# An elementwise kernel with its own semaphores: first loads ahead of the entry barrier, a single engine's wait at the end, y kept whole in SBUF

## The chip, the cores and the metric

The kernel runs on one core of a Trainium2 chip. The metric is the device time in microseconds (us) of the whole execution. Each execution also has a span, from its first recorded instruction to its last. The time is longer than the span by a part that the trace does not show: 1.77 us in the profiled run of the kernel before. This change moves that part too, to 1.33 us.

Engines are called as in the profile: PE (TensorE), DVE (VectorE), ACT (ScalarE), POOL (GpSimd), SP (SyncE).

## The reference

```python
B, S, D = 1024, 16, 512          # x, y: [B, S, D] bf16; gamma: [D] bf16
def reference(x, y, gamma):
    return x + gamma * y
```

It reads two tensors of 16.8 MB and writes one: 50.33 MB in all, for one multiply and one add per element.

## The kernel before

Each of the 128 partitions holds 128 rows of 512 elements. The work is cut in four pieces of 32 rows (4 MB each). A tile framework allocates six buffers, places the waits, and opens and closes the program with rounds in which all engines meet (barriers).

```python
    nc.gpsimd.dma_start(out=gamma_row[:], in_=gamma.unsqueeze(0))
    nc.vector.memset(ones_row[:], 1.0)
    nc.tensor.matmul(gamma_ps[:], ones_row[:], gamma_row[:], start=True, stop=True)  # gamma to all partitions
    nc.vector.tensor_copy(out=gamma_sb[:], in_=gamma_ps[:])
    io_pool = ctx.enter_context(tc.tile_pool(name="io", bufs=SLOTS))                 # SLOTS = 6
    # ... cut: lists xs and ys, the call for manual scheduling ...
    for c in range(n_pieces):                                                        # 4 pieces
        r = slice(c * PIECE, (c + 1) * PIECE)
        xt = io_pool.tile([P, PIECE, D], dt, tag="io")
        yt = io_pool.tile([P, PIECE, D], dt, tag="io")
        nc.sync.dma_start(out=xt[:], in_=xv[:, r, :])      # SP's queue
        nc.scalar.dma_start(out=yt[:], in_=yv[:, r, :])    # ACT's queue
        # ... cut: DVE: yt = yt * gamma_sb, then yt = xt + yt; xt and yt go into the lists ...
    for c in range(n_pieces):
        r = slice(c * PIECE, (c + 1) * PIECE)
        eng = nc.sync if c % 2 == 0 else nc.scalar
        eng.dma_start(out=ov[:, r, :], in_=ys[c][:])
```

(The small tiles' allocations are cut.) Six buffers hold three pieces of x and of y. The loads of the fourth piece wait for buffers: x3 is issued after the first add (40.2 us), y3 after the second (59.6 us). Below, x0 to x3, y0 to y3 and out0 to out3 are the loads and stores of the four pieces.

## Time and profile before

| | before |
|---|---|
| time, median of 3 runs (range) | 123.46 us (123.09 to 123.53) |
| profiled run: time, span | 123.22 us, 121.45 us |
| first 32 KB packet starts, last one ends | 1.76 us, 119.95 us |
| 32 KB packets: number, usual duration, in flight | 1,536, 1.213 us, 16 |
| DVE busy | 70.4 us |

The packet rows are read from the DMA packet records of the trace, which have the start, duration, size and queue of every packet. They do not name the DMA engine: with 16 packets in flight, and the page's share of 16 engines, every 16 packets are counted here as one for each engine.

These are lines of the page of the kernel before. "DMA" and "GB/s" have one value for each of 40 equal slices of the span (3.04 us each); a 9 means 90% or more busy. Part 4 is the chain of work that ended last.

```profile
span 121.5 us, 80 instructions
...
PE 0.6 (0%) x1; PEld 0.1 (0%) x1; DVE 70.4 (58%) x10; POOL 0.8 (1%) x5
...
DMA  5899999999999999999999999989898989898992
GB/s 173 378 486 389 475 399 464 399 464 421 442 432 432 410 453 410 453 399 464 410 453 410 453 410 453 345 345 518 356 507 356 507 356 507 367 496 389 475 410 108
...
## 4 chain that ended last, share of the span: by engine, by line
DMA 53%; DVE 29%; ACTq 0%; issue 0%
```

The DMA row is at 9 or 8 from the second slice to the last but one: the DMA engines bound this kernel. A sum confirms it: 1,536 packets / 16 x 1.213 us = 116.5 us, at 432 GB/s, of the 118.19 us from the first packet to the end of the last. The shortest of the 1,536 packets takes 1.211 us, so the usual duration is also the best that this trace shows; whether such a packet could be faster is not shown. Taken at this rate, there is little to win in the middle. What can be won lies before the first packet, after the last one, and in slow packets. The latter come to 1.55 us per engine over the usual duration, most of it in two places: the first packet of each engine (0.60 us over), and one round at 77.6 us (0.75 us over).

The head of the timeline (start in us, duration in us, engine; "q" is the sequencer that issues; a merged row's duration reaches from its first issue to the end of its last):

```profile
0.74 1.37 ACTq L57 DMA_DIRECT2D yt<-in_y_dram  x3
0.74 1.33 SPq L56 DMA_DIRECT2D xt<-in_x_dram  x3
...
1.22 0.61 POOL L43 DMA_DIRECT2D gamma_row<-in_gamma_dram  x1 [0.78 <-POOLq L85]
...
11.05 0.69 DVE L47 CAST gamma_sb<-gamma_ps 128x512 bf16<-128x512 f32 x1 [10.06 <-PE gamma_ps L46]
```

Both queues issue their first load at 0.74 us, after the entry barrier. The first packet starts at 1.76 us, 1.0 us later.

The end, from the view of the closing line of the program (L96), with columns count, shortest/median/longest ns, first and last start in us:

```profile
L96 SPq EVENT_SEMAPHORE  x7: 17/28/28, 120.3 to 121.4; - x7
L96 POOLq EVENT_SEMAPHORE  x4: 17/17/17, 120.7 to 121.3; - x4
...
L96 SPq DRAIN  x3: 7/7/7, 120.6 to 120.9; - x3
...
L96 DVEq EVENT_SEMAPHORE  x2: 21/21/21, 120.9 to 121.4; - x2
...
L96 POOLq EVENT_SEMAPHORE_RANGE_CLEAR  x1: 136/136/136, 121.0 to 121.0; - x1
```

SP's wait for the stores is over at 120.3 us. Then come drains, rounds of semaphores among the five engines and a clear of a range of semaphores, up to 121.4 us.

### The profile page before, as it was taken

The numbers are of one execution on the slowest core, as the hardware profiler recorded it, in microseconds if no ns is written. First come the engines' busy times: TensorE is split into PE (matmuls) and PEld (weight loads), VectorE is DVE, ScalarE is ACT, GpSimd is POOL, SyncE is SP. The second block draws the span as 40 slices with busy tenths as digits, with TensorE's granted clock in tenths as the row PEclk, the third lists the DMA queues.
The fourth block names the chain that finished last, engine by engine and source line by source line (L and its number), as shares of the span: only waits on it lengthen the run. The fifth ranks groups of instructions, "written<-read, shape, count | busy, mean of one in ns | idle before, by whom it ended". The sixth has DMA issues, their size and how long they took to land.

```text
span 121.5 us, 80 instructions
## 1 busy us (share of the span) xinstructions
PE 0.6 (0%) x1; PEld 0.1 (0%) x1; DVE 70.4 (58%) x10; POOL 0.8 (1%) x5
## 2 busy tenths in 40 slices
PE   0001000000000000000000000000000000000000
PEld 0000000000000000000000000000000000000000
DVE  0002000499999399999679999907999990000000
POOL 2000000000000000000000000000000000000000
DMA  5899999999999999999999999989898989898992
GB/s 173 378 486 389 475 399 464 399 464 421 442 432 432 410 453 410 453 399 464 410 453 410 453 410 453 345 345 518 356 507 356 507 356 507 367 496 389 475 410 108
DMA packets 1760, 50.33 MB, mean 414 GB/s; under 512 B 224, under 2 KB 224, under 8 KB 224
## 3 DMA queue, kind: packets, MB, share of 16 engines
q10 hardware_dynamic: 864, 25.17, 48.7%
q1 hardware_dynamic: 864, 25.17, 48.6%
q0 software_dynamic: 32, 0.00, 0.0%
HBM read 33.56 MB, written 16.78 MB: 414 GB/s over the span
## 4 chain that ended last, share of the span: by engine, by line
DMA 53%; DVE 29%; ACTq 0%; issue 0%
DMA yt<-in_y_dram 53%; DVE yt L58 14%; DVE yt L64 14%; ACTq L57 0%
## 5 line engine op out<-in xcount | busy, mean ns | idle before, releaser
L58 DVE TENSOR_TENSOR yt<-yt,gamma_sb 128x16384 bf16<-128x16384 bf16 x4 | 34.8, 8692 | 18.9 <-DMA yt<-in_y_dram 18.9
L64 DVE TENSOR_TENSOR yt<-xt,yt 128x16384 bf16<-128x16384 bf16 x4 | 34.8, 8692 | 0.1
L47 DVE CAST gamma_sb<-gamma_ps 128x512 bf16<-128x512 f32 x1 | 0.7, 692 | 10.1 <-PE gamma_ps L46 10.1
L44 DVE MEMSET ones_row<- 1x128 bf16 x1 | 0.2, 165 | 0.8 <-PEq L85 0.8
L46 PE MATMUL gamma_ps<-gamma_row,ones_row 1*128 1x512 bf16 x1 | 0.6, 579 | 10.4 <-DMA gamma_row<-in_gamma_dram 10.4
L43 POOL DMA_DIRECT2D gamma_row<-in_gamma_dram x1 | 0.6, 607 | 0.8 <-POOLq L85 0.8
L46 PEld LDWEIGHTS <-ones_row 1*128 1x128 bf16 x1 | 0.1, 98 | 1.0 <-DVE ones_row L44 1.0
L85 POOL MEMSET const-bfloat16-1.0<- 128x1 bf16 x1 | 0.1, 97 | 0.0
L85 POOL MEMSET const-float32-0.0<- 128x1 f32 x1 | 0.1, 93 | 0.2 <-issue 0.2
L85 POOL MEMSET const-float32-1.0<- 128x1 f32 x1 | 0.1, 94 | 0.0
L85 POOL MEMSET const-uint8-127<- 128x1 uint8 x1 | 0.1, 94 | 0.0
## 6 DMA issues: line engine op xcount, KB each, us to landing
yt<-in_y_dram ACTq DMA_DIRECT2D x4, 4096.0 KB, 32.1
xt<-in_x_dram SPq DMA_DIRECT2D x4, 4096.0 KB, 40.5
out_dram<-yt SPq DMA_DIRECT2D x2, 4096.0 KB, 49.0
out_dram<-yt ACTq DMA_DIRECT2D x2, 4096.0 KB, 31.1
gamma_row<-in_gamma_dram POOLq DMA_DIRECT2D x1, 1.0 KB, 9.2
```

The lines of the kernel that those rows point to most:

```text
L43: nc.gpsimd.dma_start(out=gamma_row[:], in_=gamma.unsqueeze(0))
L44: nc.vector.memset(ones_row[:], 1.0)
L46: nc.tensor.matmul(gamma_ps[:], ones_row[:], gamma_row[:], start=True, stop=True)
L47: nc.vector.tensor_copy(out=gamma_sb[:], in_=gamma_ps[:])
L58: nc.vector.tensor_tensor(out=yt[:], in0=yt[:], in1=gamma_sb[:, None, :].to_broadcast([P, PIECE, D]), op=mybir.AluOpType.mult,)
L64: nc.vector.tensor_tensor(out=yt[:], in0=xt[:], in1=yt[:], op=mybir.AluOpType.add)
L85: nc = _bacc.Bacc("TRN2", target_bir_lowering=False, num_devices=1)
```

## The change

The intent is to put the DMA-free parts at both ends out of the way.

- The tile program is closed empty at the start; the kernel is written behind it with its own semaphores (counters on which engines wait), each of which the waiting engine counts back to zero.
- The first five loads (gamma, x0, x1, y0, y1) are moved to the front of the program, ahead of the entry barrier.
- At the end only SP waits, for the four stores.
- y has room for all four pieces in SBUF (the memory in which the buffers lie), x for two; gamma is loaded by ACT instead of POOL.

```diff
+def _take(sem, n, eng):
+    return eng.wait_ge(sem, n).then_inc(sem, -n)
...
+    tc.close()
+    tc.compile()
...
-    io_pool = ctx.enter_context(tc.tile_pool(name="io", bufs=SLOTS))
+    y_sb = nc.alloc_sbuf_tensor("y_sb", [P, rows, D], dt).ap()
+    xs = [nc.alloc_sbuf_tensor(f"x{i}", [P, PIECE, D], dt).ap() for i in range(2)]
...
-    nc.gpsimd.dma_start(out=gamma_row[:], in_=gamma.unsqueeze(0))
+    first.append(load(nc.scalar, gamma_row, gamma.unsqueeze(0), s_gamma))
...
+    first.append(load(nc.sync, xs[0], xv[:, piece(0), :], s_x[0]))
+    first.append(load(nc.sync, xs[1], xv[:, piece(1), :], s_x[1]))
+    _take(s_sp, 1, nc.sync)                                    # first add done
+    load(nc.sync, xs[0], xv[:, piece(2), :], s_x[2])
+    _take(s_sp, 1, nc.sync)                                    # second add done
+    load(nc.sync, xs[1], xv[:, piece(3), :], s_x[3])
+    nc.sync.dma_start(out=ov[:, piece(0), :], in_=y_sb[:, piece(0), :]).then_inc(s_out_sp, 16)
... (cut: out2 on SP; y0 to y3, then out1 and out3 on ACT; the two passes of DVE)
+    _take(s_out_sp, 32, nc.sync)
+    _take(s_out_act, 32, nc.sync)
+
+    main = nc.main_func.blocks[0].instructions
+    names = {i.ins.name for i in first}
+    for b in nc.main_func.blocks[1:]:
+        for i in [i for i in b.instructions if i.name in names]:
+            b.instructions.remove(i)
+    for k, i in enumerate(first):
+        main.insert(1 + k, i.ins)
```

More of the change, by code (lines that the diff above doesn't have):

```diff
@@ L1 @@
-from contextlib import ExitStack
 import concourse.bass as bass
@@ L5 @@
 from concourse import mybir
-from concourse._compat import with_exitstack
 PIECE = 32
-SLOTS = 6
-@with_exitstack
+MULT, ADD = mybir.AluOpType.mult, mybir.AluOpType.add
+def _take(sem, n, eng):
+    return eng.wait_ge(sem, n).then_inc(sem, -n)
 def kernel(
-    ctx: ExitStack,
     tc: tile.TileContext,
@@ L30 @@
     rows = N // P
-    n_pieces = rows // PIECE
+    n = rows // PIECE
     dt = xf.dtype
@@ L36 @@
     ov = of.rearrange("(p n) d -> p n d", p=P)
-    const_pool = ctx.enter_context(tc.tile_pool(name="const", bufs=1))
-    gamma_row = const_pool.tile([1, D], dt)
-    ones_row = const_pool.tile([1, P], dt)
-    gamma_sb = const_pool.tile([P, D], dt)
-    psum_pool = ctx.enter_context(tc.tile_pool(name="psum", bufs=1, space=bass.MemoryType.PSUM))
-    nc.gpsimd.dma_start(out=gamma_row[:], in_=gamma.unsqueeze(0))
-    nc.vector.memset(ones_row[:], 1.0)
-    gamma_ps = psum_pool.tile([P, D], mybir.dt.float32)
@@ L46 @@
-    nc.tensor.matmul(gamma_ps[:], ones_row[:], gamma_row[:], start=True, stop=True)
-    nc.vector.tensor_copy(out=gamma_sb[:], in_=gamma_ps[:])
-    io_pool = ctx.enter_context(tc.tile_pool(name="io", bufs=SLOTS))
-    xs, ys = [], []
-    ctx.enter_context(tc.manual_schedule())
-    for c in range(n_pieces):
-        r = slice(c * PIECE, (c + 1) * PIECE)
-        xt = io_pool.tile([P, PIECE, D], dt, tag="io")
-        yt = io_pool.tile([P, PIECE, D], dt, tag="io")
-        nc.sync.dma_start(out=xt[:], in_=xv[:, r, :])
-        nc.scalar.dma_start(out=yt[:], in_=yv[:, r, :])
-        nc.vector.tensor_tensor(
-            out=yt[:],
-            in0=yt[:],
-            in1=gamma_sb[:, None, :].to_broadcast([P, PIECE, D]),
-            op=mybir.AluOpType.mult,
-        )
-        nc.vector.tensor_tensor(out=yt[:], in0=xt[:], in1=yt[:], op=mybir.AluOpType.add)
-        xs.append(xt)
-        ys.append(yt)
@@ L67 @@
-    for c in range(n_pieces):
-        r = slice(c * PIECE, (c + 1) * PIECE)
-        eng = nc.sync if c % 2 == 0 else nc.scalar
-        eng.dma_start(out=ov[:, r, :], in_=ys[c][:])
+    gamma_row = nc.alloc_sbuf_tensor("gamma_row", [1, D], dt).ap()
+    ones_row = nc.alloc_sbuf_tensor("ones_row", [1, P], dt).ap()
+    gamma_sb = nc.alloc_sbuf_tensor("gamma_sb", [P, D], dt).ap()
+    y_sb = nc.alloc_sbuf_tensor("y_sb", [P, rows, D], dt).ap()
+    xs = [nc.alloc_sbuf_tensor(f"x{i}", [P, PIECE, D], dt).ap() for i in range(2)]
@@ new lines, with piece, load @@
+    gamma_ps = nc.alloc_psum_tensor("gamma_ps", [P, D], mybir.dt.float32).ap()
+    sem = nc.alloc_semaphore
+    s_gamma, s_ones, s_ps, s_dve = sem("s_gamma"), sem("s_ones"), sem("s_ps"), sem("s_dve")
+    s_x = [sem(f"s_x{c}") for c in range(n)]
+    s_y = [sem(f"s_y{c}") for c in range(n)]
+    s_sp, s_act = sem("s_sp"), sem("s_act")
+    s_out_sp, s_out_act = sem("s_out_sp"), sem("s_out_act")
+    def piece(c):
+        return slice(c * PIECE, (c + 1) * PIECE)
+    first = []
+    def load(eng, dst, src, s):
+        return eng.dma_start(out=dst, in_=src).then_inc(s, 16)
@@ new lines @@
+    first.append(load(nc.scalar, gamma_row, gamma.unsqueeze(0), s_gamma))
+    nc.vector.memset(ones_row, 1.0).then_inc(s_ones, 1)
+    _take(s_ones, 1, nc.tensor)
+    _take(s_gamma, 16, nc.tensor)
+    nc.tensor.matmul(gamma_ps, ones_row, gamma_row, start=True, stop=True).then_inc(s_ps, 1)
+    _take(s_ps, 1, nc.vector)
+    nc.vector.tensor_copy(out=gamma_sb, in_=gamma_ps).then_inc(s_dve, 1)
+    _take(s_dve, 1, nc.vector)
+    first.append(load(nc.sync, xs[0], xv[:, piece(0), :], s_x[0]))
+    first.append(load(nc.sync, xs[1], xv[:, piece(1), :], s_x[1]))
@@ new lines @@
+    _take(s_sp, 1, nc.sync)
[3 more added lines that the diff above has]
+    nc.sync.dma_start(out=ov[:, piece(0), :], in_=y_sb[:, piece(0), :]).then_inc(s_out_sp, 16)
+    _take(s_sp, 1, nc.sync)
+    nc.sync.dma_start(out=ov[:, piece(2), :], in_=y_sb[:, piece(2), :]).then_inc(s_out_sp, 16)
+    for c in range(n):
+        i = load(nc.scalar, y_sb[:, piece(c), :], yv[:, piece(c), :], s_y[c])
+        if c < 2:
+            first.append(i)
@@ new lines @@
+    _take(s_act, 1, nc.scalar)
+    nc.scalar.dma_start(out=ov[:, piece(1), :], in_=y_sb[:, piece(1), :]).then_inc(s_out_act, 16)
+    _take(s_act, 1, nc.scalar)
+    nc.scalar.dma_start(out=ov[:, piece(3), :], in_=y_sb[:, piece(3), :]).then_inc(s_out_act, 16)
+    for c in range(n):
+        yt = y_sb[:, piece(c), :]
+        _take(s_y[c], 16, nc.vector)
+        nc.vector.tensor_tensor(
+            out=yt, in0=yt, in1=gamma_sb[:, None, :].to_broadcast([P, PIECE, D]), op=MULT
+        ).then_inc(s_dve, 1)
+        _take(s_x[c], 16, nc.vector)
+        _take(s_dve, 1, nc.vector)
+        i = nc.vector.tensor_tensor(out=yt, in0=xs[c % 2], in1=yt, op=ADD)
+        if c == 0:
+            i.then_inc(s_sp, 1)
+        elif c == 1:
+            i.then_inc(s_dve, 1)
+            _take(s_dve, 1, nc.vector)
+            nc.vector.sem_inc(s_sp, 1)
+            nc.vector.sem_inc(s_act, 1)
+        else:
+            i.then_inc(s_sp if c == 2 else s_act, 1)
```

## The prediction

> **What bounds the kernel now.** The DMA engines. The page gives a span of 121.5 us, 50.33 MB moved, and a DMA row at 9 or 8 in nearly every slice; VectorE is busy 70.4 us (58%). In the trace's packet records the 1,536 packets of 32 KB take 1.21 us each, 16 at a time: 1536/16 x 1.213 = 116.5 us, or 432 GB/s.[...] The first such packet starts at 1.76 us, the last ends at 119.95 us: 118.2 us with 16 in flight throughout. Two things stretch them: the first packet of each engine takes about 1.9 us, and one round at 77.6 us, the first writes, about 1.95 us.
>
> - Ahead: the timeline has both first loads issued at 0.74 us, after the entry barrier (SP's waits show 0.7 us for it); first bytes about 1.0 us later.
> - Behind: SP's wait for the stores ends at about 120.3 us; then drains, two all-engine rounds of semaphores and a range clear run to 121.45 us: 1.15 us.
>
> **What the change does.**
> 1. Gamma, x0, x1, y0, y1 are issued before the entry barrier: SP's first at about 0.05 us in place of 0.74. Worth 0.65 to 0.7 us, all critical, since every transfer queues behind. Gamma now heads ACT's queue, so y0 is issued about 0.4 us after x0; x0 alone fills the engines meanwhile (at the end of this trace one queue alone keeps 1.21 us per packet). Cost about 0.
> 2. The closing drains, barriers and clear go; SP's waits with decrements stay (28 ns each). Worth 1.0 to 1.1 us, all critical.
> 3. y whole in SBUF: y3 is issued at once instead of at 59.6 us, x2 at 40.2 us instead of at once. x2 comes into SP's queue about when x1's last packet goes, and y2 fills any gap[...]. y3 lands about 2 us earlier (82.8 before), so the last add ends near 98 us instead of 100.3. No gain: out0 and out2 hold the engines then. Worth 0 +- 0.3 us.
> 4. Gamma by ACT, not POOL: off the path (VectorE waits from 11.7 to 22.8 us for y0).
> 5. VectorE's eight passes of 8.69 us: unchanged, hidden.
>
> **Sum.** 123.46 - 0.68 - 1.07 = 121.7 us; I say 121.65, range 121.0 to 122.3. Faster by over 2%: 0.11; within 2%: 0.87; slower: 0.02. Predicted span: 119.7 us.
>
> **What would show it right or wrong.**
> - Step 1: first DMA issue near 0.05 us, first 32 KB packet near 1.05 us.
> - Step 2: the trace ends within 0.2 us of the end of SP's wait.
> - Step 3: 32 KB packets still 1.21 us, first to last 118.2 us (117.7 to 118.7); DMA at 9 with no hollow slice near 41, 60 or 98 us.
>
> **What would make it wrong.** The 1.8 us between measured time and span of the same run (123.22 against 121.5) may hold work that changes with the program's start or ending. Reads and writes no longer meet in the same way, so slow rounds may be more, fewer or longer. If x2 or x3 comes late and both queues run dry, a hole of about 1 us appears. If the first access has a fixed start after launch whatever is issued, step 1 gives nothing.

## The result

| | before | after |
|---|---|---|
| time, median of 4 runs (range) | 123.41 us (123.09 to 123.53) | 121.23 us (121.17 to 121.28) |
| profiled run: time | 123.22 us | 121.17 us |
| its span | 121.45 us | 119.84 us |
| time minus span | 1.77 us | 1.33 us |
| first 32 KB packet starts | 1.76 us | 1.01 us |
| from there to the end of the last | 118.19 us | 118.37 us |
| from there to the end of the span | 1.50 us | 0.46 us |

The ratio is 0.9827 (95% interval 0.9808 to 0.9846). By the ratio the change is faster by 1.5 to 1.9%, inside the "within 2%" to which the prediction gave 0.87.

The page of the changed kernel, the same lines as above (slices of 3.00 us):

```profile
span 119.8 us, 90 instructions
...
PE 0.6 (0%) x1; PEld 0.1 (0%) x1; DVE 70.3 (59%) x10; POOL 0.2 (0%) x4
...
DMA  8999998989898989898999989999999999989994
GB/s 274 427 427 448 405 470 361 514 350 525 350 525 350 525 350 525 350 492 383 437 437 427 448 372 405 405 394 481 394 481 394 448 427 438 437 383 470 405 470 197
...
## 4 chain that ended last, share of the span: by engine, by line
DVE 7%; issue 0%
```

The first and the last slice are fuller; in between the row is as full as before. Part 4 needs care. It says "DVE 7%" and nothing of DMA, though the kernel is as DMA-bound as before. In both kernels the chain's last piece is the last add, which ends 21 us before the end of the span in the kernel before and 25 us here; the stores behind it are in neither chain. From the last add the view went back to 0.68 us in the kernel before, through the loads, but here it stopped at once: a wait here is an instruction of its own that also lowers the semaphore, and the view did not follow the chain back through it. For the bound, the DMA row and the packets are to be read, not the chain.

The head of the timeline of the changed kernel:

```profile
0.00 0.86 SPq L62 DMA_DIRECT2D x<-in_x_dram  x2
0.12 0.53 ACTq L62 DMA_DIRECT2D gamma_row<-in_gamma_dram  x1
...
0.69 2.75 ACTq L62 DMA_DIRECT2D y_sb<-in_y_dram  x4
...
5.42 0.69 DVE L71 CAST gamma_sb<-gamma_ps 128x512 bf16<-128x512 f32 x1 [2.56 <-DVEq L12]
```

Its waits, from the view of line L12, the wait in `_take` (columns as for the end of before):

```profile
L12 DVEq EVENT_SEMAPHORE  x15: 21/21/21, 5.3 to 86.2; - x15
L12 SPq EVENT_SEMAPHORE  x5: 17/17/17, 41.8 to 119.8; - x5
...
L12 ACTq EVENT_SEMAPHORE  x2: 17/17/17, 59.5 to 95.0; - x2
```

SP issues x0 at 0.00 us, and its last semaphore instruction, at 119.8 us, is the end of the program. VectorE's and ACT's last waits lie far ahead of it. The closing rounds did not quite disappear: closing the tile program empty puts them at its place, near the start. They are on the line of that close, L29:

```profile
L29 POOLq EVENT_SEMAPHORE  x4: 17/17/17, 2.1 to 2.5; - x4
L29 SPq DRAIN  x3: 7/7/7, 2.0 to 2.3; - x3
...
L29 SPq EVENT_SEMAPHORE  x2: 17/17/17, 2.2 to 2.5; - x2
```

They run at 2.0 to 2.5 us, while the first loads are already moving.

The two profiled runs differ by 2.05 us, and the table gives the sum: start -0.75, transfers +0.18, end inside the span -1.04, and outside the span -0.44. The last term was not predicted at all.

### The profile page after: what moved, and what is told of

It is laid out like the page before. It is cut to its first block, busy times and chain, and to the rows that moved or that the text cites. A ratio compares the mean times of both kernels' runs of the same rounds, so it can differ in the third digit from the quotient of the medians.

```text
span 119.8 us, 90 instructions
## 1 busy us (share of the span) xinstructions
PE 0.6 (0%) x1; PEld 0.1 (0%) x1; DVE 70.3 (59%) x10; POOL 0.2 (0%) x4
## 5 line engine op out<-in xcount | busy, mean ns | idle before, releaser
L98 DVE TENSOR_TENSOR y_sb<-y_sb,gamma_sb 128x16384 bf16<-128x16384 bf16 x4 | 34.8, 8690 | 18.9 <-DVEq L12 18.9
L104 DVE TENSOR_TENSOR y_sb<-x,y_sb 128x16384 bf16<-128x16384 bf16 x4 | 34.8, 8692 | 0.6
```

The costliest lines, as they stand in the source:

```text
L98: nc.vector.tensor_tensor(out=yt, in0=yt, in1=gamma_sb[:, None, :].to_broadcast([P, PIECE, D]), op=MULT).then_inc(s_dve, 1)
L104: i = nc.vector.tensor_tensor(out=yt, in0=xs[c % 2], in1=yt, op=ADD)
```

## The experiments

Each kernel was run on one chip beside the kernel before, whose median there was 123.3 to 123.4 us. Three groups of four shared a chip each: the control, early issue alone, no early issue and all engines held; the closing rounds, the storage of before, the earlier store and the cut load; the other three runs about the end, and gamma. All results were correct. The question for each term: which part of the change gives it?

### The control

The changed kernel itself.

> The changed kernel itself, as the control on this chip. Expected 121.2 us (ratio 0.982 to 0.984 to the kernel before), span 119.8 us, and 1.3 to 1.4 us between measured time and span, where the kernel before had 1.77 us.

Measured: 120.94 us (120.87 to 121.19), ratio 0.9814 (0.9799 to 0.9829); time minus span 1.29 to 1.37 us in its five runs, against 1.72 to 1.82 us in the eleven runs of the kernel before beside it. The difference outside the span is real and steady. (Except for the profiled runs, spans are on record to 0.1 us, so single values of time minus span are good to 0.05 us.)

### Early issue alone, in the kernel before

```diff
     with _tile.TileContext(nc) as tc:
         ...
+    main, body = nc.main_func.blocks[0].instructions, nc.main_func.blocks[1].instructions
+    loads = [i for i in body if type(i).__name__ == "InstDMACopy" and i.engine != _mybir.EngineType.Pool][:4]
+    for k, i in enumerate(loads):
+        body.remove(i)
+        main.insert(1 + k, i)
```

> The kernel before with x0, x1, y0 and y1 issued ahead of the entry barrier, nothing else. Theory: the early issue gives its 0.7 us by itself and no more; first issue near 0.0 us, span 120.7 to 120.8 us, and 1.77 us between time and span stay, so 122.7 us. Rival: the part of the gain that lies outside the span (0.44 us) belongs to the start; then that difference falls to about 1.33 us and the time is 122.25 us. Other rival: the start is fixed by the launch; then 123.4 us.

Measured: 122.55 us, ratio 0.9938 (0.9925 to 0.9952). The head of its timeline:

```profile
0.00 1.73 SPq L56 DMA_DIRECT2D xt<-in_x_dram  x3
0.12 1.65 ACTq L57 DMA_DIRECT2D yt<-in_y_dram  x3
```

The first packet starts at 0.99 us, and time minus span stays at 1.72 to 1.82 us. So moving four instructions in the kernel before gives 0.77 us by itself, and the part outside the span does not belong to the start.

### The changed kernel without early issue

```diff
+    first = []
     main = nc.main_func.blocks[0].instructions
```

> The changed kernel with no load moved: all loads stay behind the entry barrier and behind the two rounds of semaphores that the empty tile program left there. Theory: those rounds, hidden in the changed kernel, now stand on the path: first load issued near 1.3 us (entry barrier 0.7 plus two rounds of 0.3), span 121.1 us, time minus span still 1.33 us, time 122.5 us, so 1.3 us over the changed kernel. Rival (the part outside the span belongs to the start): time minus span 1.77 us and time 122.9 us. If the rounds cost nothing at the start: 121.9 us.

Measured: 122.46 us, ratio 0.9932 (0.9919 to 0.9946); time minus span 1.28 to 1.37 us. The head of its timeline:

```profile
1.38 0.85 SPq L62 DMA_DIRECT2D x<-in_x_dram  x2
1.39 0.53 ACTq L62 DMA_DIRECT2D gamma_row<-in_gamma_dram  x1
...
1.95 1.89 ACTq L62 DMA_DIRECT2D y_sb<-in_y_dram  x4
```

The first load goes out at 1.38 us: later than in the kernel before (0.74), because the displaced closing rounds now stand ahead of it. On the same chip it is 1.52 us slower than the changed kernel, where 1.3 was expected; the later issue is 1.38 of it. Even so it is 0.86 us faster than the kernel before: what the rounds cost at the start (0.64 us of later issue) is less than what is won at the end. The early issue hides them.

### All engines held to the end

```diff
     _take(s_out_act, 32, nc.sync)
+    for k, eng in enumerate((nc.scalar, nc.vector, nc.tensor, nc.gpsimd)):
+        s = sem(f"s_end{k}")
+        nc.sync.sem_inc(s, 1)
+        _take(s, 1, eng)
```

> The changed kernel, but ACT, VectorE, TensorE and POOL each wait at their end for a semaphore that SP raises after its wait for the stores: no drains, no rounds, no clear, only all five engines ending together. Theory: the 0.44 us outside the span comes from four engines having ended long before; then time minus span returns to about 1.77 us with the span at 119.9 to 120.0 us, time 121.7 us. Rival: it comes from the early start or from the dropped clear; then time minus span stays at 1.33 us and the time is 121.3 us.

Measured: 122.03 us, ratio 0.9899 (0.9884 to 0.9913). Its waits:

```profile
L12 DVEq EVENT_SEMAPHORE  x16: 21/21/21, 5.3 to 120.1; - x16
L12 SPq EVENT_SEMAPHORE  x5: 17/17/17, 41.9 to 119.9; - x5
L12 PEldq EVENT_SEMAPHORE  x3: 51/51/51, 2.9 to 120.1; - x3
L12 ACTq EVENT_SEMAPHORE  x3: 17/17/17, 59.6 to 120.0; - x3
L12 POOLq EVENT_SEMAPHORE  x1: 17/17/17, 120.2 to 120.2; - x1
```

All five engines now end between 119.9 and 120.2 us, and time minus span is 1.83 to 1.88 us: the part outside the span is back, with the early start kept and no clear put back. So this part depends on which engines end late. The total is 1.09 us over the changed kernel on the same chip: 0.5 outside the span, 0.3 for the extra semaphores (last packet to end of span 0.72 us against 0.44 in the profiled runs), and a rest of about 0.3 us. In the two profiles the transfers differ by 0.39 us (118.48 against 118.09), but the changed kernel's own two profiles already differ by 0.28, so this rest has no shown cause.

### Which engine?

POOL alone held (the loop over `(nc.gpsimd,)`):

> The changed kernel with POOL alone waiting at its end for SP's wait for the stores. After the run in which four engines waited, time minus span was 1.83 to 1.88 us, without them 1.29 to 1.38. Theory A (one engine's late end is enough, and it is POOL's): time minus span 1.75 to 1.9 us, time 121.6 to 121.8 us. Theory B (it is another engine's, or it needs all of them): time minus span 1.33 us, time 121.1 to 121.3 us.

Measured: 121.75 us, ratio 0.9882 (0.9861 to 0.9904), time minus span 1.85 to 1.91 us. From its waits (L12), POOL ends last and ACT long before:

```profile
L12 SPq EVENT_SEMAPHORE  x5: 17/17/17, 41.9 to 120.3; - x5
...
L12 ACTq EVENT_SEMAPHORE  x2: 17/17/17, 59.6 to 95.6; - x2
L12 POOLq EVENT_SEMAPHORE  x1: 17/17/17, 120.4 to 120.4; - x1
```

ACT, VectorE and TensorE held (the loop over `(nc.scalar, nc.vector, nc.tensor)`):

> The complement: ACT, VectorE and TensorE wait at their ends for SP, POOL does not. Theory A (POOL alone): time minus span stays at 1.33 us, time 121.2 to 121.4 us with a span about 0.2 us longer than the changed kernel's. Theory B (another engine, or the number of engines): time minus span 1.75 us or more, time 121.7 to 122.0 us.

Measured: 121.68 us, ratio 0.986 (0.9837 to 0.9884), time minus span 1.62 to 1.67 us. Neither theory said that: POOL is enough, but the others count too.

The last two waits on ACT in place of SP:

```diff
-    _take(s_out_sp, 32, nc.sync)
-    _take(s_out_act, 32, nc.sync)
+    _take(s_out_sp, 32, nc.scalar)
+    _take(s_out_act, 32, nc.scalar)
```

> The changed kernel with its last two waits on ACT in place of SP, so ACT ends last. If what lies outside the span belongs to whichever engine ends last and is alike for all, 121.2 us within 0.15 and time minus span 1.33 us. If it differs by engine, time minus span moves, by up to 0.5 us, and the time with it; a lower one would be a better kernel.

Measured: 121.47 us, ratio 0.9849 (0.9829 to 0.9869), time minus span 1.47 to 1.55 us.

Together: what follows the last instruction takes about 1.33 us when only SP ends last, 1.5 for ACT, 1.65 for ACT, VectorE and TensorE together, and 1.88 for POOL. SP is the best of those tried. The runs show that it depends on the engine; what the engines do in that time, no trace here shows. VectorE and TensorE were not held alone.

### Closing rounds put back

```diff
     _take(s_out_act, 32, nc.sync)
+    nc.all_engine_barrier()
+    nc.all_engine_barrier()
```

> The changed kernel with two all-engine barrier rounds put back behind SP's last wait (drain and semaphores of every engine, as at the kernel before's end; no range clear). Theory: the span grows by the two rounds, 0.6 to 1.0 us, and time minus span returns to 1.77 us, so 122.3 to 122.6 us (1.1 to 1.4 over the changed kernel). Rival (the closing rounds overlap something else): at most 0.3 us more, 121.5 us.

Measured: 122.36 us, ratio 0.9915 (0.9892 to 0.9937). Last packet to end of span: 1.07 us, against 0.46; time minus span 1.76 to 1.80 us. The ratio is 0.009 to 0.010 over the changed kernel's, or 1.1 to 1.2 us. Putting the rounds back costs in both places, about 0.6 us in the span and 0.45 outside. That is 0.6 of the 1.04 us won inside the span: the range clear and the remaining drains and semaphores of the old ending were not put back, so the other 0.4 us is read from the old ending's trace and not tested by itself. (The profiled run had also 118.84 us of transfers, 0.5 more than the changed kernel, with 1.02 us of slow packets shortly before the first store; the changed kernel's own two profiles differ by 0.28 us in their transfers.)

### The storage of before

Three buffers for x and three for y; x2 issued at once, y3 only after the second add:

```diff
-    y_sb = nc.alloc_sbuf_tensor("y_sb", [P, rows, D], dt).ap()
-    xs = [nc.alloc_sbuf_tensor(f"x{i}", [P, PIECE, D], dt).ap() for i in range(2)]
+    xs = [nc.alloc_sbuf_tensor(f"x{i}", [P, PIECE, D], dt).ap() for i in range(3)]
+    ys = [nc.alloc_sbuf_tensor(f"y{i}", [P, PIECE, D], dt).ap() for i in range(3)]
+    xs.append(xs[0])
+    ys.append(xs[1])
... (cut: x2 not waiting, y3 behind the wait for the second add, ys[c] for y_sb)
```

> The changed kernel with the storage of the kernel before: six buffers, x2 issued at once, y3 waiting for the second add and taking x1's buffer; early issue and short ending kept. Theory (y kept whole is worth nothing): 121.2 us within 0.2, 32 KB packets still 1.21 us with 16 in flight, one round of slow packets where writes begin. Rival (y kept whole gains by issuing y3 early): 121.6 us or more.

Measured: 121.30 us, ratio 0.9831 (0.9806 to 0.9856), against 0.9827 and 0.9814 for the changed kernel. Transfers take 118.61 us, with 16 packets in flight. Keeping y whole is worth nothing that these runs can see.

### The first store issued earlier

out0 directly behind x2, at 42.3 us, in place of behind x3 at 59.8 us:

```diff
     load(nc.sync, xs[0], xv[:, piece(2), :], s_x[2])
+    nc.sync.dma_start(out=ov[:, piece(0), :], in_=y_sb[:, piece(0), :]).then_inc(s_out_sp, 16)
     _take(s_sp, 1, nc.sync)
     load(nc.sync, xs[1], xv[:, piece(3), :], s_x[3])
-    nc.sync.dma_start(out=ov[:, piece(0), :], in_=y_sb[:, piece(0), :]).then_inc(s_out_sp, 16)
```

> The changed kernel with the store of piece 0 issued right after x2, at about 42 us, in place of behind x3 at 59.8 us. Theory: the slow round, about 0.8 to 0.9 us per engine, is a one-off that comes where writes first meet reads; it moves to about 55 to 62 us, when the store's first packets go, and the total stays at 121.2 us within 0.2. The last add may end later (x3 lands later, behind the store), but the engines are kept busy by other stores. Rival: mixing reads and writes costs over the whole stretch in which they are mixed; then packets over 1.25 us are spread over tens of us and the time rises by 0.5 us or more.

Measured: 121.60 us, ratio 0.9858 (0.9831 to 0.9885). On the slow round the theory held in the main: it moved with the store, to 62.5 to 66.5 us, and cost 0.77 us per engine (0.87 us at 73.1 to 76.9 us in the changed kernel). In this run it is a one-off, not a tax on mixing. One thing no theory had: the slow packets are loads, not stores. Counted along the queues, this is so in the profiles of both kernels and of ten experiments (the cut load and the moved gamma, below, left out): the first slow packet starts 2.8 to 3.5 us before the first store packet. What slows them is not shown. On the total the theory missed by 0.2 us, and its last clause is why. x3 came behind the store, so the last add ended at 109.0 us and out3 was issued at 109.15 us; the windows of this kernel (us; busy time by engine; then clock, DMA share, GB/s) show the gap in the middle line:

```profile
core 0: us, PE busy (x) PEld busy (x) DVE busy (x) POOL busy (x), PEclk, DMA share, GB/s
100.00:108.00 8.00, 0.00 (x0) 0.00 (x0) 7.65 (x1) 0.00 (x0) 1.00 1.01 438
108.00:112.00 4.00, 0.00 (x0) 0.00 (x0) 1.04 (x1) 0.00 (x0) 1.00 0.71 303
112.00:118.00 6.00, 0.00 (x0) 0.00 (x0) 0.00 (x0) 0.00 (x0) 1.00 1.02 437
```

The same windows of the changed kernel, which do not have it:

```profile
100.00:108.00 8.00, 0.00 (x0) 0.00 (x0) 0.00 (x0) 0.00 (x0) 1.00 1.03 446
108.00:112.00 4.00, 0.00 (x0) 0.00 (x0) 0.00 (x0) 0.00 (x0) 1.00 0.95 410
112.00:118.00 6.00, 0.00 (x0) 0.00 (x0) 0.00 (x0) 0.00 (x0) 1.00 0.99 426
```

In the packets, none is in flight from 109.46 to 110.00 us: 0.54 us, which is the whole difference of the transfers (118.91 against 118.37 us).

### The first load cut in two

x0 as its first 16 partitions, then the other 112:

```diff
-    first.append(load(nc.sync, xs[0], xv[:, piece(0), :], s_x[0]))
+    first.append(load(nc.sync, xs[0][:16], xv[:16, piece(0), :], s_x[0]))
+    first.append(load(nc.sync, xs[0][16:], xv[16:, piece(0), :], s_x[0]))
```

> The changed kernel with x0 cut in two loads: its first 16 partitions (one row for each engine), then the other 112. Theory A: the time from issue to first packet (1.0 us) grows with the size of the load; then the first packet starts at 0.6 to 0.8 us and the time falls by 0.2 to 0.4 us, to 120.9 us. Theory B: it is a fixed latency; first packet at 1.0 us, time 121.2 us within 0.15.

Measured: 131.82 us, ratio 1.0689 (1.066 to 1.0719). The first packet started at 1.02 us, so the time from issue to first packet did not shrink (Theory B), but both theories missed what came next. Windows of this kernel:

```profile
0.00:28.00 28.00, 0.58 (x1) 0.10 (x1) 0.86 (x2) 0.20 (x4) 1.00 0.99 245
28.00:60.00 32.00, 0.00 (x0) 0.00 (x0) 23.15 (x3) 0.00 (x0) 1.00 0.99 422
60.00:130.00 70.00, 0.00 (x0) 0.00 (x0) 46.20 (x6) 0.00 (x0) 1.00 0.99 428
```

For the first 28 us, in which nearly all of the cut x0 is loaded (its last packet ends at 29.9 us), the DMA share is 0.99, but only 245 GB/s move. The 16 packets of the small piece take 2.6 to 4.5 us each (the first 16 of the changed kernel take 1.6 to 2.0). In stretches of 4 us the median is then 2.4 us, and from 8 us on 1.6 to 2.1 us, for the packets of y0 beside x0 too. After x0 has landed, packets are back at 1.21 us. What slows the packets until then is not shown. "Busy" here is no sign of throughput: share and GB/s must be read together.

### gamma behind the first loads of y

```diff
-    first.append(load(nc.scalar, gamma_row, gamma.unsqueeze(0), s_gamma))
...
         if c < 2:
             first.append(i)
+        if c == 1:
+            first.append(load(nc.scalar, gamma_row, gamma.unsqueeze(0), s_gamma))
```

> The changed kernel with the gamma load behind y0 and y1 on ACT's queue in place of ahead of them; y0 is issued 0.57 us earlier for it. Theory: a queue's transfers start in the order of issue, so gamma lands only with y1, near 41 us, and VectorE starts then in place of at 24 us; the loads of x2 and x3 and all stores come later, the engines run dry, 126 to 129 us. Rival (gamma's place is free, as its 1 KB interleaves anyhow): 121.0 to 121.3 us, with y0 landing a little earlier.

Measured: 131.17 us, ratio 1.0632 (1.061 to 1.0653): the theory's direction, and more than its range. From the page (slices of 3.24 us):

```profile
span 129.7 us, 90 instructions
...
DVE  0000000000000999999999998999999999900000
...
DMA  9799799899999989983999007999989989989987
GB/s 323 333 475 485 344 465 485 374 434 485 414 394 485 445 364 485 445 364 162 394 414 485 0 0 162 404 404 485 434 374 485 445 364 485 445 384 465 445 384 303
```

gamma arrives with y1: the matmul that needs it starts at 41.37 us (4.69 in the changed kernel), the first multiply at 43.05 us (24.24). x2 and x3 then wait for the adds, and the engines run dry: no packet is in flight from 60.20 to 61.65 and from 72.46 to 79.23 us. The queue served in order of issue here: gamma's packet, issued at 1.02 us behind y0 and y1, starts at 40.38 us. 1 KB at this place of the queue cost 10 us. The kernel before had gamma on a queue of its own; in the changed one it must not stand behind y0 and y1. The engines have no packet for 8.2 us in all, and from first to last packet it is 10.0 us longer than in the changed kernel, more than the estimate of 126 to 129 us allowed.

No version tried beats the changed kernel. One was left out: gamma back on POOL in the changed kernel. So that part was not tested alone.

## Why the prediction was right, point by point

- **What bounds the kernel: right.** 32 KB packets stay at 1.213 us, 16 in flight. From first to last 118.2 us was predicted (117.7 to 118.7), 118.37 measured. One detail was misread: the slow round at 77.6 us is not "the first writes" but loads of y3, 3.1 us before the first store packet.
- **Step 1, early issue: right.** 0.65 to 0.7 us predicted; the first packet came 0.75 us earlier, and the early issue alone gave 0.77 us in the kernel before.
- **Step 1, "y0 is issued about 0.4 us after x0": the size was off, at no cost.** gamma's issue takes 0.53 us, so y0 was issued 0.69 us after x0, and its first packet came at 5.24 us, behind three packets of x0 on each engine. The issue is not all of it: y0's first packet came 4.5 us after its issue with gamma ahead of it, and 2.6 to 2.8 us after it in the three kernels in which y0 heads its queue (the kernel before, early issue alone, gamma moved). The first multiply started at 24.24 us instead of 22.80.
- **Step 2, the closing rounds: right in size, incomplete in place.** 1.0 to 1.1 us predicted in the span, 1.04 measured. The rounds did not go; they moved to 2.0 to 2.5 us, and without early issue the first load is issued at 1.38 us.
- **Step 3, y whole: right.** Worth 0 +- 0.3 us predicted; the storage of before in the changed program measured the same within its interval. The detail "x2 comes into SP's queue about when x1's last packet goes" was wrong: x1's last packet ended at 37.04 us, x2 was issued at 41.87 and its first packet came at 45.39. The other half of the sentence saved it: y2 filled the gap, with 16 packets in flight all along. y3's last packet ended at 74.8 us, where the prediction had about 81, and the last add at 95.0 us (98 predicted); no gap came of either.
- **The sum: 121.65 us predicted, 121.23 measured; the span 119.7 predicted, 119.84 measured.** The term missed is the part outside the span, taken as unchanged: it fell by 0.44 us, from 1.77 to 1.33. The prediction named it as a risk, not as an effect. Holding the other four engines to the end brought it back (1.83 to 1.88 us), and the runs with other engines last showed that it depends on which engine ends last.
- **"If the first access has a fixed start after launch": it has not.** The first packet came about 1.0 us after the first issue, wherever the issue stood (0.74 to 1.76, 0.00 to 1.01, 1.38 to 2.38).

## What to carry to other kernels

When the DMA engines are full from first to last packet, the remaining time is at the two ends: issue the first loads ahead of everything that does not feed them (0.77 us in the kernel before), end with the fewest engines and let the others end early (outside the span 1.33 us with SP alone last, 1.83 to 1.88 with all five), and compare time minus span as well as spans. Work that cannot be dropped (closing rounds, gamma) can be moved under the first transfers, but what the compute needs first should be issued first: behind y0 and y1, gamma started 39 us after its issue, and the time was 131.17 us. A load that is cut to start sooner should be measured before it is kept: the one cut into 16 and 112 partitions started no sooner (1.02 us) and had a full DMA row at 245 GB/s, where 422 to 428 moved once it was over.

## What the traces showed of issue and first packet

- From the end of the issuing instruction to the start of the first 32 KB packet it was 0.62 to 0.64 us in four kernels (the changed kernel, the kernel before, no early issue, early issue alone). From the start of the issue it was 1.0 us (1.01, 1.02, 1.00, 0.99), and cutting the first load to 16 packets did not shorten it (1.02).
- A queue that joined busy engines waited longer: y0 from issue to first packet 2.6 to 2.8 us at the head of its queue and 4.5 us (0.69 to 5.24) behind gamma, x2 3.5 us (41.87 to 45.39), against 1.0 us on idle engines.
- The one-off cost shortly before the first store was about 0.7 to 1.0 us of longer load packets per engine in the profiles of both kernels and of ten experiments (the cut load and the run with gamma behind y1 left out).
